# A frequency-domain mixing stage spread beside a feed-forward pipeline: two helper stages run further ahead, in finer steps, with two sums on another engine

## The chip, the cores and the metric

The kernel runs on one core of one Trainium2 chip. The core has a matrix engine (PE, TensorE), a vector engine (DVE, VectorE), an activation engine (ACT, ScalarE), a second elementwise engine (POOL, GpSimd) and a queue engine (SP, SyncE) that here only issues DMAs. Each engine works through its own instructions in the order in which the program gives them, and waits for the others through semaphores. The metric is the time on the device in microseconds, the median over several executions.

## The reference

The input x has 8 batches of 3008 rows and 256 columns. Each column is transformed along the rows, multiplied by a filter and transformed back; the result goes through two matrix products with x - tanh(x) between them.

```python
def _attn_ref(x, filt_r, filt_i):            # x (8, 3008, 256)
    X = np.fft.rfft(x, axis=1)
    F = (filt_r + 1j * filt_i)[None, :, :]   # (1505, 256)
    y = np.fft.irfft(X * F, n=x.shape[1], axis=1)
    return y.astype(np.float32)

def _moe_ref(x, w_in, w_out):                # x (24064, 256), w_in (256, 2048), w_out (2048, 256)
    h = x @ w_in
    g = h - np.tanh(h)
    return (g @ w_out).astype(np.float32)
```

## The kernel before

The transform of length 3008 = 64 x 47 is done in factors, as matrix products with constant matrices, and a batch goes through four stages:

- **first**, function `first`: 12 steps. A step loads two residues of x and the matrix f (SP queue), does 2 products on PE (line 296), copies the result out of PSUM on ACT (line 297) and stores it to the DRAM tensor ct1 (ACT queue). The loads of a step are asked for two steps ahead.
- **middle**, function `middle`: 7 slots. For a slot, `forth` does the 47-point transform (line 328, two pairs of products; the first pair is copied by ACT, the second is added to and subtracted from it on DVE, lines 333 and 334); `filtered` multiplies by the filter, with two products on POOL (lines 343 and 346), a difference and a sum into nn (lines 348 and 349), and a last sum and difference into xy (lines 351 and 352); `back` does the inverse 47-point transform (line 362, two pairs), copies each pair out on ACT (line 365) and stores it to the DRAM tensor ct2 (ACT queue). The slot's rows of ct1 (a2) and of the filter (ft) are loaded one slot ahead on SP. `back` of slot g is run within slot g+1.
- **last**, function `last`: per group of residues the final transform on PE (line 449, into pu), two copies by ACT, and four differences by `combine` (lines 463 to 466).
- **the feed-forward part**: 192 units U = 0 to 191; four units u = 0 to 3 make a group c = 0 to 5, six groups a batch p. Units are named c.u below. The two matrix products are done with seven products in place of eight. `up(U)` makes h in three PSUM banks x, y, z (line 483), from which DVE and ACT form the four blocks of h (lines 489, 506, 523, 531, 539); `shrink(U-1)` applies the approximated x - tanh(x) (ACT lines 554, 557, 565; DVE lines 561, 568) and the four differences t, on POOL, called t-combines (lines 463 to 466); `down(U-2)` does the second product (line 615) and, in each fourth unit, sums up the outputs, which are transposed on DVE (line 668) and stored by SP (line 695).

The order is written by hand: within a unit `up` calls back into `shrink`, `down` and, at five points, into t(k), k = 0 to 4. The point t(k) of unit c.u has the position 20c + 5u + k, so a batch has 120 positions. There one step of a helper stage is emitted on all engines at once: in units u = 3, at k = 0 and 2, a step of `last` for the next group; otherwise the next step of `first` or `middle` whose planned position has been reached. The t-combines of a unit are emitted between t(3) and t(4), just behind DVE's second line 568; DVE's line 539 stands behind t(4), line 506 behind the next unit's t(0), and the unit's first line 561 ahead of t(1).

While batch p runs, the plan puts first(p+1) at positions 0.24 to 32 and middle(p+1), in 51 steps, at 38 to 103. Batch 0's own first and middle stages run in a prologue that also converts weights; there the products of `filtered` are on DVE, its sums on POOL. The start of the next batch's loads and the two PSUM banks of the helper stages ("t", and "y" at k = 1, 2, 3) are set in the same loop.

Of the kernel before, what the change touches and what calls it, by code (L numbers as in the profile page):

```python
# [17 lines left out]
BATCH, SEQ, DM = 8, 3008, 256  # L18
# [8 lines left out]
NC = NH // CH  # L27
NX = NH // XH
SLOTS = [(a, min(SG, NA - a)) for a in range(0, NA, SG)]
KM = SG * NH  # L30
KL = SLOTS[-1][1] * NH
EARLY = 0

SMALL = 0.36
FACTORS = [(0.28138768672943115, 0.18210311233997345, 0.5012423992156982),
           (0.28138768672943115, -0.6558710336685181, 0.19358105957508087)]

FIRST, MID = (0.24, 32), (38, 103)

S, K = 0.6389930153911744, 0.3476472316053873  # L40
A, B = 0.18659689165196622, -0.6846325776203513
# [51 lines left out]
def kernel(  # L93
# [10 lines left out]
    V, G, ACT = nc.vector, nc.gpsimd, nc.scalar  # L104
# [232 lines left out]
    def filtered(g, xy, ft, by, by2):  # L337

        n = SLOTS[g][1] * NH
        ab = xy.rearrange("p (x v) c -> p x v c", v=2)  # L340
        fv = ft[0:n].rearrange("p (x v) c -> p x v c", v=2)
        nn = tr.tile([KM, 4, DM], F32, tag="nn", bufs=1, name="nn")[0:n]
        by.tensor_mul(nn.rearrange("p (x v) c -> p x v c", v=2), ab,  # L343
                      fv[:, :, 0:1].to_broadcast([n, 2, 2, DM]))
        yield
        by.tensor_mul(ab, ab, fv[:, :, 1:2].to_broadcast([n, 2, 2, DM]))  # L346
        yield
        by2.tensor_sub(nn[:, 0:4:3], nn[:, 0:4:3], xy[:, 1:3])  # L348
        by2.tensor_add(nn[:, 1:3], nn[:, 1:3], xy[:, 0:4:3])
        yield  # L350
        by2.tensor_add(xy[:, 0:2], nn[:, 0:2], nn[:, 2:4])  # L351
        by2.tensor_sub(xy[:, 2:4], nn[:, 0:2], nn[:, 2:4])  # L352
        yield

    def back(b, g, xy, z):
# [13 lines left out]
    def middle(b, z):  # L369

        a2, ft = {0: load_a2(b, 0)}, {0: load_ft(0)}
        waiting = iter(())
        yield
        for g in range(len(SLOTS)):
            if g + 1 < len(SLOTS):
                a2[g + 1], ft[g + 1] = load_a2(b, g + 1), load_ft(g + 1)
            there = forth(g, a2.pop(g), z)
            xy = next(there)
            yield
            next(there)  # L380
            done = filtered(g, xy, ft.pop(g), G, G)
            next(done)
            yield
            next(done)
            yield
            for _ in waiting:
                yield
            for _ in done:
                yield
            waiting = back(b, g, xy, z)  # L390
        yield
        yield
        for _ in waiting:
            yield
# [392 lines left out]
    with tc.tile_pool(name="tr", bufs=2) as tr, tc.manual_schedule():  # L787
        with tc.tile_pool(name="pro", bufs=1) as pro, \
# [81 lines left out]
            for g in range(last_g + 1):  # L870
# [3 lines left out]
                xy = next(there)  # L874
# [3 lines left out]
                done = filtered(g, xy, fts.pop(g), V, G)  # L878
# [6 lines left out]
                if g == last_g - 1:  # L885
                    fs = first(1, z1)
# [3 lines left out]
            for _ in waiting:  # L890
                pass
            e2s[0] = load_e2(*groups[0])
            for _ in range(EARLY):
                next(fs)
            for w in (ws, ws_gap):
                for _ in w:
                    pass
# [5 lines left out]
        with tc.tile_pool(name="dn", bufs=2) as dn, \  # L903
                tc.tile_pool(name="ps", bufs=1, space=bass.MemoryType.PSUM) as ps:

            quarter, latest = [1], ["t"]

            def zd(name, shape):
                latest[0] = "y" if quarter[0] in (1, 2, 3) and latest[0] == "t" else "t"
                return ps.tile(shape, F32, tag=latest[0], bufs=1, name=name)  # L910

            psums.append(zd)

            y_sums = dn.tile([128, 2 * 4 * len(groups)], F32, bufs=1, name="y_sums")

            def psl(shape, tag):
                return ps.tile(shape, F32, tag=tag, bufs=1, name="pt")

            def tiles1(k, dtype, n):

                tag, bufs = {"raw": ("ft", 2), "it": ("xy", 2), "pt": ("nn", 1), "st": ("e1", 2),
                             "ft": ("a2", 2)}[k]
                return tr.tile([128, n], dtype, tag=tag, bufs=bufs, name=k)

            def filters_d():
                zero = tr.tile([128, 2 * DM], F32, tag="a2", bufs=2, name="zero")
                G.memset(zero, 0.0)
                n = len(SLOTS) - 1
                nc.sync.dma_start(dram(filt_d, 2 * DM, [[KM * 4 * DM, n], [4 * DM, SG],
                                                        [1, 2 * DM]]), zero[0:n * SG])  # L930
                nc.sync.dma_start(dram(filt_d, (n * KM * 4 + 2) * DM, [[4 * DM, 1], [1, 2 * DM]]),
                                  zero[0:1])
                yield
                for g in range(len(SLOTS)):
                    for v, row, n, src in filter_rows(g):
                        G.dma_start(dram(filt_d, ((g * KM + row) * 4 + v) * DM,
                                         [[4 * DM, n], [1, DM]]), src)
                        yield

            bound = bounded()  # L940
            late, copies = weights_slow(tiles1, range(6, 8)), filters_d()
            total = 4 * len(groups)
            for _ in last(0, z1):
                pass
            next(late)
            for U in range(total + 2):
                i, u = divmod(U, 4)
                if U < total:
                    p, c = groups[i]
                    if c == 0 and u == 0:  # L950
                        steps, done = [], 0 if p else EARLY
                        if p + 1 < BATCH:
                            steps = [FIRST[0] + (FIRST[1] - FIRST[0]) * (k - done) / (NX - done)
                                     for k in range(NX)]
                            n_m = 7 * len(SLOTS) + 2
                            steps += [MID[0] + (MID[1] - MID[0]) * k / n_m for k in range(n_m)]
                            ms = None
                    if u == 0 and i + 1 < len(groups) and c + 1 < NC:
                        e2s[i + 1] = load_e2(*groups[i + 1])
                    if u == 2 and i + 1 < len(groups) and c + 1 == NC:  # L960
                        assert done == len(steps)
                        e2s[i + 1] = load_e2(*groups[i + 1])
                    if u == 0 and c + 1 == NC and p + 2 < BATCH:
                        fs = first(p + 2, z1)
                        next(fs)
                    if u == 2 and i + 1 < len(groups):
                        lasts = last(i + 1, z1)
                sh = shrink(U - 1) if 0 <= U - 1 < total else iter(())
                dw = down(U - 2) if 0 <= U - 2 < total else iter(())

                def d():

                    next(dw, None)

                def e():

                    next(dw, None)

                def s():

                    next(sh, None)

                def t(k):

                    nonlocal ms, done
                    quarter[0] = k
                    if k == 2 and stores:
                        store(*stores.pop())
                    store_some(4)
                    if U >= total:  # L990
                        return
                    pos = 20 * c + 5 * u + k
                    if u == 3 and k in (0, 2) and i + 1 < len(groups):
                        next(lasts)
                    elif done < len(steps) and steps[done] <= pos:
                        next(fs if done < NX else ms)
                        done += 1
                        if done == NX and ms is None:
                            ms = middle(p + 1, z1)
                            next(ms)  # L1000
                    next(late, None)
                    if k:
                        next(copies, None)

                if U < total:
                    if U == total - 1:
                        one = tr.tile([128, 128], F32, tag="x", bufs=3, name="one_sb")
                        nc.sync.dma_start(one, one_d)
                        ones = cst.tile([128, 1], F32, name="ones")
                        G.memset(ones, 1.0)  # L1010
                    up(U, d, e, s, t)
                else:
                    for k in range(5):
                        s()
                        s()
                        d()
                        if U == total + 1 and k in (0, 2):
                            next(bound)
                        e()
                        t(k)  # L1020
            for w in stores:
                store(*w)
            store_some(len(outs))
# [36 lines left out]
```

## Time and profile before

| | |
|---|---|
| median of 3 runs | 2919.11 us (2917.21 to 2925.43) |
| profiled execution, own time | 2923.08 us |
| its span | 2921.2 us |
| mean granted PE clock | 0.974 |
| instructions | 37028 |
| DMA moved | 215.48 MB, mean 74 GB/s |

The page gives the busy time of each engine and its share of the span, then the span in 40 equal slices with the busy share of each in tenths, and the chain of work that ended last. Views by line, by wait and by stretch of time come from the same trace. Line numbers are those of the kernel before; in the changed kernel the same lines stand a little lower or higher.

### The profile page before, as it was taken

What the parts mean: (1) busy time and instruction counts of PE and PEld (TensorE: products, weight loads), DVE (VectorE), ACT (ScalarE), POOL (GpSimd) and SP (SyncE); (2) the same over time, 40 slices, a digit from 0 to 9 for tenths busy, and PEclk for the clock granted to TensorE, in tenths of its full rate; (3) what the DMA queues carried; (4) which work ended last, traced back from release to release, by engine and by line L of the source; (5) the groups of instructions that cost most, each with busy time, mean ns of one, the idle gap of its engine ahead of it and who ended that gap; (6) DMA issues with size and microseconds to landing.
All of it is one profiled execution on the core that took longest, in us unless ns stands there. A gap on an engine that the chain in (4) does not pass through costs nothing.

```text
span 2921.2 us, 37028 instructions
## 1 busy us (share of the span) xinstructions
PE 2739.2 (94%) x12830; PEld 2373.4 (81%) x12830; DVE 2010.2 (69%) x2171; ACT 1764.4 (60%) x2583; POOL 2124.7 (73%) x1503
## 2 busy tenths in 40 slices
PE   4599999999999999999999999999999999999998
PEld 3388788988789887988779887898878988799886
DVE  5877766577665676657766677657776677677776
ACT  1156566666566665666656665666666666566665
POOL 5858995489944997559965699647995489855553
PEclk7699999999999999999999999999999999999999
DMA  9443322333123321233213322233322333111010
GB/s 249 117 151 89 76 54 53 101 81 81 42 63 98 91 63 42 76 103 73 58 40 100 91 66 58 52 107 73 80 58 52 103 73 84 26 28 35 19 26 17
DMA packets 341639, 215.48 MB, mean 74 GB/s; under 512 B 227736, under 2 KB 300988, under 8 KB 341251
## 3 DMA queue, kind: packets, MB, share of 16 engines
q1 hardware_dynamic: 296851, 154.15, 22.5%
q10 hardware_dynamic: 39504, 50.61, 5.5%
q0 software_dynamic: 5088, 8.28, 1.1%
q8 instruction: 103, 1.69, 0.3%
q14 instruction: 93, 0.76, 0.1%
HBM read 137.83 MB, written 78.12 MB: 74 GB/s over the span
## 4 chain that ended last, share of the span: by engine, by line
PE 50%; POOL 28%; DVE 10%; issue 5%; ACT 4%; DMA 2%; SPq 0%; ACTq 0%; POOLq 0%; DVEq 0%
PE o L615 21%; PE x L483 13%; PE z L483 6%; PE y L483 4%; POOL t L466 4%; DVE h L561 4%; POOL t L464 3%; POOL t L465 3%; POOL t L463 3%; POOL xy L346 2%; PE pf L296 2%; PE pu L449 2%; POOL nn L343 2%; POOL xy L352 2%; POOL nn L348 2%
## 5 line engine op out<-in xcount | busy, mean ns | idle before, releaser
L561 DVE TENSOR_TENSOR h<-h,y 128x1024 f32<-128x1024 f32 (+1 forms) x384 | 617.8, 1609 | 295.2 <-ACT y L557 295.2
L615 PE MATMUL o<-t,wd 128*128 128x256 f32 (+1 forms) x3072 | 790.4, 380 | 14.0 <-POOL t L465 7.1
L615 PEld LDWEIGHTS o<-t,wd 128*128 128x128 f32 x3072 | 586.8, 192 | 97.1 <-POOL t L465 13.7
L568 DVE SCALAR_TENSOR_TENSOR h<-sq,h 128x1024 f32<-128x1024 f32 (+1 forms) x384 | 595.7, 1551 | 99.2 <-ACT sq L565 93.2
L483 PE MATMUL x<-tu,wu 128*128 128x256 f32 (+1 forms) x2304 | 591.2, 379 | 3.1 <-ACT u L489 3.1
L615 PE MATMUL o<-h,wd 128*128 128x256 f32 (+1 forms) x2304 | 584.8, 376 | 4.6 <-DVE h L568 4.6
L463 POOL TENSOR_TENSOR t<-h 128x512 f32<-128x512 f32 (+1 forms) x190 | 245.3, 1291 | 444.4 <-DVE h L568 349.2
L483 PEld LDWEIGHTS x<-tu,wu 128*128 128x128 f32 x2304 | 435.9, 192 | 62.7 <-issue 7.9
L615 PEld LDWEIGHTS o<-h,wd 128*128 128x128 f32 x2304 | 433.7, 190 | 57.2 <-DVE h L568 8.3
L565 ACT ACTIVATE sq<-y,near_b 128x1024 f32<-128x1024 f32 (+1 forms) x384 | 435.1, 1133 | 9.2 <-DVE h L568 2.9
L554 ACT ACTIVATE y<-h 128x1024 f32<-128x1024 f32 (+1 forms) x384 | 397.5, 1035 | 13.3 <-ACT a L297 5.7
L557 ACT ACTIVATE y<-y 128x1024 f32<-128x1024 f32 (+1 forms) x384 | 399.7, 1041 | 6.3
L489 ACT COPY s<-x 128x512 f32<-128x512 f32 (+1 forms) x192 | 110.8, 577 | 424.8 <-PE x L483 424.4
L466 POOL TENSOR_TENSOR t<-t,h 128x512 f32<-128x512 f32 (+1 forms) x190 | 341.3, 1796 | 0.0
L489 ACT COPY u<-x 128x512 f32<-128x512 f32 (+1 forms) x384 | 220.7, 575 | 196.5 <-PE x L483 191.1
L465 POOL TENSOR_TENSOR t<-h 128x512 f32<-128x512 f32 (+1 forms) x190 | 277.6, 1461 | 0.0
L464 POOL TENSOR_TENSOR t<-h,t 128x512 f32<-128x512 f32 (+1 forms) x190 | 262.6, 1382 | 14.9
L523 DVE TENSOR_TENSOR h<-z,u 128x512 f32<-128x512 f32 (+1 forms) x192 | 128.5, 669 | 166.4 <-ACT u L489 165.8
L483 PE MATMUL x<-ut,wu 128*128 128x256 f32 (+1 forms) x768 | 202.2, 386 | 36.2 <-DVE h L531 35.0
L362 PE MATMUL pe<-xy,mats_sb 120*120 120x256 f32 (+1 forms) x448 | 132.6, 426 | 78.4 <-POOL xy L351 78.4
L483 PEld LDWEIGHTS x<-ut,wu 128*128 128x128 f32 x768 | 139.7, 191 | 76.2 <-DVE h L531 61.2
L506 DVE TENSOR_TENSOR h<-y,s 128x512 f32<-128x512 f32 (+1 forms) x192 | 130.1, 677 | 99.0 <-PE y L483 93.8
(116 smaller groups left out, 3688.7 us busy)
## 6 DMA issues: line engine op xcount, KB each, us to landing
e<-ct SPq DMA_DIRECT2D x48, 512.0 KB, 4.8
a<-ct SPq DMA_DIRECT2D x48, 480.0 KB, 4.9
ct<-e ACTq DMA_DIRECT2D x96, 240.0 KB, 2.5
ct<-a ACTq DMA_DIRECT2D x84, 256.0 KB, 3.1
x_sb<-in_x_dram SPq DMA_DIRECT2D x161, 128.0 KB, 3.3
ft<-filt SPq DMA_DIRECT2D x42, 480.0 KB, 6.3
out_dram<-ot SPq DMA_DIRECT2D x1248, 16.0 KB, 1.5
gt<-g SPq DMA_DIRECT2D x48, 256.0 KB, 3.2
```

Source lines behind the costliest of these rows:

```text
L463: by.tensor_sub(t[0], b[0][1], b[0][0])
L464: by.tensor_sub(t[1], b[1][1], t[0])
L465: by.tensor_sub(t[2], b[1][1], b[0][1])
L466: by.tensor_sub(t[3], t[1], b[1][0])
L483: nc.tensor.matmul(bank[:, k], wu[:, q - 1, (2 * u + k) * 128:(2 * u + k + 1) * 128], rhs[q - 1], start=(first and k == 0), stop=True, ski ...
L489: ACT.copy(t, X)
L554: ACT.activation(y[k], ht[k], AF.Arctan, scale=S)
L557: ACT.activation(y[k], y[k], AF.Square, accum_out=y_sums[:, 2 * U + k // 2:2 * U + k // 2 + 1])
L561: V.tensor_mul(ht[k], ht[k], y[k])
L565: ACT.activation(sq[k], y[k], AF.Square, bias=near_b, scale=A)
L568: V.scalar_tensor_tensor(out=ht[k], in0=sq[k], scalar=K, in1=ht[k], op0=ALU.add, op1=ALU.mult)
L615: nc.tensor.matmul(product(q), wd[:, q - 1, (2 * u + k) * 128: (2 * u + k + 1) * 128], rhs[q - 1][:, k], start=(u == 0 and k == 0 and q == ...
```

## The change

Both helper stages run one batch further ahead in part. While batch p runs, first(p+2) and middle(p+1) are both spread evenly over positions 0.2 to 102; while batch 0 runs, first(1) takes positions 0.2 to 15, first(2) 15 to 30, and middle(1) 30 to 102. The steps of both are merged in order of position, and one is emitted at a point. `middle` gets a further pause in each slot, between the sum and difference of `forth` and the first product of `filtered`, and one more in the last slot; one pause behind the last slot goes: 58 steps in place of 51. The last sum and difference of `filtered` are done on DVE, in the stages and in the prologue. The generators of the stages to come are made, and their first loads asked for, at position 105 of batch p, for middle(p+2) and first(p+3).

```diff
@@ filtered
         by2.tensor_sub(nn[:, 0:4:3], nn[:, 0:4:3], xy[:, 1:3])
         by2.tensor_add(nn[:, 1:3], nn[:, 1:3], xy[:, 0:4:3])
         yield
-        by2.tensor_add(xy[:, 0:2], nn[:, 0:2], nn[:, 2:4])
-        by2.tensor_sub(xy[:, 2:4], nn[:, 0:2], nn[:, 2:4])
+        V.tensor_add(xy[:, 0:2], nn[:, 0:2], nn[:, 2:4])
+        V.tensor_sub(xy[:, 2:4], nn[:, 0:2], nn[:, 2:4])
         yield
@@ middle
             next(there)
+            yield
             done = filtered(g, xy, ft.pop(g), G, G)
             next(done)
             yield
             next(done)
             yield
             for _ in waiting:
+                yield
+            next(done)
+            yield
+            if g + 1 == len(SLOTS):
                 yield
             for _ in done:
                 yield
             waiting = back(b, g, xy, z)
-        yield
         yield
         for _ in waiting:
             yield
@@ the plan
-FIRST, MID = (0.24, 32), (38, 103)
+LEAD, LAG = 30, 102
...
-                        steps, done = [], 0 if p else EARLY
-                        if p + 1 < BATCH:
-                            steps = [FIRST[0] + (FIRST[1] - FIRST[0]) * (k - done) / (NX - done)
-                                     for k in range(NX)]
-                            n_m = 7 * len(SLOTS) + 2
-                            steps += [MID[0] + (MID[1] - MID[0]) * k / n_m for k in range(n_m)]
-                            ms = None
+                        steps = planned(p)
...
+            def planned(p):
+                def spread(n, lo, hi, *what):
+                    return [(lo + (hi - lo) * k / n, *what, k) for k in range(n)]
+                n_m = 8 * len(SLOTS) + 2
+                f = [spread(NX, *((0.2, LEAD / 2) if b == 1 else (LEAD / 2, LEAD) if b == 2
+                                  else (0.2, LAG)), firsts, b, first)
+                     for b in ([1, 2] if p == 0 else [p + 2]) if b < BATCH]
+                m = [spread(n_m, LEAD if p == 0 else 0.2, LAG, mids, b, middle)
+                     for b in [p + 1] if b < BATCH]
+                return sorted(sum(f + m, []), key=lambda s: s[0])
...
-                    if u == 0 and c + 1 == NC and p + 2 < BATCH:
-                        fs = first(p + 2, z1)
-                        next(fs)
+                    if u == 1 and c + 1 == NC:
+                        for gens, ahead, what in ((mids, 2, middle), (firsts, 3, first)):
+                            if p + ahead < BATCH:
+                                gens[p + ahead] = what(p + ahead, z1)
+                                next(gens[p + ahead])
...
-                    elif done < len(steps) and steps[done] <= pos:
-                        next(fs if done < NX else ms)
-                        done += 1
-                        if done == NX and ms is None:
-                            ms = middle(p + 1, z1)
-                            next(ms)
+                    elif steps and steps[0][0] <= pos:
+                        _, gens, b, what, n = steps.pop(0)
+                        if b not in gens:
+                            gens[b] = what(b, z1)
+                            next(gens[b])
+                        next(gens[b])
```

More of the change, by code (lines that the diff above doesn't have):

```diff
@@ L31 @@
 KL = SLOTS[-1][1] * NH
-EARLY = 0
 SMALL = 0.36
@@ L892 @@
             e2s[0] = load_e2(*groups[0])
-            for _ in range(EARLY):
-                next(fs)
             for w in (ws, ws_gap):
@@ L945 @@
             next(late)
+            def planned(p):
[8 more added lines that the diff above has]
+                return sorted(sum(f + m, []), key=lambda s: s[0])
+            firsts, mids = {1: fs}, {}
             for U in range(total + 2):
@@ L960 @@
                     if u == 2 and i + 1 < len(groups) and c + 1 == NC:
-                        assert done == len(steps)
+                        assert not steps
                         e2s[i + 1] = load_e2(*groups[i + 1])
-                    if u == 0 and c + 1 == NC and p + 2 < BATCH:
-                        fs = first(p + 2, z1)
-                        next(fs)
+                    if u == 1 and c + 1 == NC:
[3 more added lines that the diff above has]
+                                next(gens[p + ahead])
                     if u == 2 and i + 1 < len(groups):
@@ L983, in t @@
                 def t(k):
-                    nonlocal ms, done
                     quarter[0] = k
```

## The prediction

> **What bounds the kernel now.** I read the page first: busy shares, slices, chain.
>
> ```profile
> span 2921.2 us, 37028 instructions
> ...
> PE 2739.2 (94%) x12830; PEld 2373.4 (81%) x12830; DVE 2010.2 (69%) x2171; ACT 1764.4 (60%) x2583; POOL 2124.7 (73%) x1503
> ...
> POOL 5858995489944997559965699647995489855553
> ...
> PE 50%; POOL 28%; DVE 10%; issue 5%; ACT 4%; DMA 2%; SPq 0%; ACTq 0%; POOLq 0%; DVEq 0%
> ```
>
> PE is busy almost throughout, yet the chain that ended last runs on POOL for 28% of the span. POOL's digits go up to 9 once per batch. So I cut the span at the copy of line 531, which DVE makes once in each of the 192 units: batch 0, batch 1, batch 6, batch 7 (to its last copy).
>
> ```profile
> 156.20:511.20 355.00, 333.78 (x1563) 287.52 (x1564) 255.63 (x274) 217.14 (x318) 285.88 (x215) 0.99 0.31 79
> 511.20:860.10 348.90, 337.62 (x1602) 293.78 (x1601) 237.35 (x250) 219.51 (x322) 262.76 (x174) 0.99 0.29 73
> ...
> 2258.50:2606.70 348.20, 336.92 (x1598) 293.16 (x1597) 238.21 (x250) 218.97 (x321) 262.80 (x174) 0.99 0.28 68
> 2606.70:2890.80 284.10, 283.56 (x1370) 252.60 (x1369) 211.37 (x228) 191.33 (x275) 162.71 (x125) 1.00 0.11 23
> ```
>
> The columns after the length are PE, PEld, DVE, ACT and POOL busy, granted clock, DMA share, GB/s. Batches 1 to 6 take (2606.70 - 511.20) / 6 = 349.3 each. Batch 7 has no first or middle stage beside it and shows what a batch costs without them. The same view by groups of four units: five groups of batch 2, its group 4, five groups of batch 7, its group 4.
>
> ```profile
> 860.10:1155.90 295.80, 284.54 (x1352) 247.71 (x1351) 201.58 (x211) 184.61 (x271) 234.93 (x152) 0.99 0.31 76
> 1089.60:1155.90 66.30, 59.31 (x265) 48.44 (x266) 43.89 (x43) 37.45 (x54) 59.08 (x36) 0.97 0.18 41
> 2606.70:2854.05 247.35, 246.87 (x1201) 220.69 (x1200) 181.97 (x196) 166.50 (x240) 142.19 (x110) 1.00 0.12 24
> 2803.60:2854.05 50.45, 50.40 (x241) 44.19 (x240) 37.03 (x40) 33.93 (x49) 29.25 (x22) 1.00 0.08 11
> ```
>
> A bare batch is 247.35 + 50.45 = 297.8, with PE never idle. In group 4 of batch 2 PE idles 7 of 66.30 us and POOL works 59.08. Its late middle stage waits for POOL:
>
> ```profile
> 1494.45 0.59 PE L615 MATMUL o<-t,wd 128*128 128x256 f32 x2
> 1498.52 1.58 PE L362 MATMUL pe<-xy,mats_sb 48*48 48x256 f32 x4 [3.48 <-POOL xy L351]
> ...
> 1508.44 0.81 PE L483 MATMUL z<-ut,wu 128*128 128x256 f32 x3
> ```
>
> PE stood still 3.48 us until POOL's sum of line 351, and was then slow. Undisturbed, four matmuls follow the next four after 0.86 us (z at 2804.05, x at 2804.91, rows further down), 0.216 each.
>
> ```profile
> L296 PE MATMUL pf<-x_sb,f 128*128 128x256 f32 x336 | 87.9, 384 | 1.0 <-DVE h L506 0.7 <-ACT a L297 0.2
> ...
> L362 PE MATMUL pe<-xy,mats_sb 120*120 120x256 f32 (+1 forms) x448 | 132.6, 426 | 78.4 <-POOL xy L351 78.4
> ```
>
> A first stage is 336 / 7 = 48 matmuls, a middle stage 448 / 8 = 56 in line 362 and by the code as many in line 328. At 0.216 that is 10.4 and 24.2, so PE needs 297.8 + 34.6 = 332.4 for a full batch and 349.3 - 332.4 = 17 are lost. Between 1498.52 and 1508.44 PE ran 28 matmuls, worth 6.0 us, in 9.9: this one event costs 3.48 + 3.9 = 7.4. It is in every batch, since it is in the order of the code.
>
> **The change part by part.** Middle work on POOL and DVE:
>
> ```profile
> L343 POOL TENSOR_TENSOR nn<-xy,ft 120x1024 f32<-120x1024 f32 x42 | 122.7, 2922 | 7.6 <-DVE xy L334 6.0
> L346 POOL TENSOR_TENSOR xy<-xy,ft 120x1024 f32<-120x1024 f32 x42 | 117.8, 2805 | 2.1
> ...
> L352 POOL TENSOR_TENSOR xy<-nn 120x512 f32<-120x512 f32 x48 | 82.5, 1719 | 0.0
> L348 POOL TENSOR_TENSOR nn<-nn,xy 120x512 f32<-120x512 f32 x48 | 82.2, 1711 | 12.5 <-DVE xy L346 12.0
> L351 POOL TENSOR_TENSOR xy<-nn 120x512 f32<-120x512 f32 x48 | 81.7, 1701 | 2.6
> L349 POOL TENSOR_TENSOR nn<-nn,xy 120x512 f32<-120x512 f32 x48 | 75.7, 1577 | 0.0
> ...
> L333 DVE TENSOR_TENSOR xy<-pa,xy 120x512 f32<-120x512 f32 x48 | 32.8, 682 | 25.6 <-PE pa L328 24.4
> ```
>
> A slot (seven per batch) costs POOL 12.4 now; the two last sums, 1.70 + 1.72 = 3.4, go to DVE. POOL falls from 262.8 to 239 of some 341 us. The steps go from 65 of a batch's 120 positions to 102, so POOL's load is level: about 40 of each 57 us group, nearer to batch 7's 29 of 50 than to 59 of 66. No form like the new DVE sums is in the stages of the trace; line 333 (0.68, one operand from PSUM) is nearest, the POOL row is the far end. I take 0.69: 7 x 1.4 = 9.7 us of DVE per batch, which is 68% busy, so beside PE's work unless DVE has to wait.
>
> Line 362 needs the sums of a slot five steps later, at 1.76 positions each about 25 us. So the 7.4 go, and with them a good part of the other 9.6 lost beside POOL at its limit; I keep 4 (ends 1 and 8). What is late next is DVE: its sums now wait for line 349, and DVE runs in order. From the plan's numbers I placed the seven pairs. In five slots POOL reaches lines 348 and 349 well before DVE reaches the sums. In slot 5 of batches 1 to 5 POOL's pair falls at the last position of a unit, behind the four t-combines, and DVE's at the first position of the next, ahead of line 506. A bare unit, to lay this on:
>
> ```profile
> 2793.63 1.28 POOL L463 TENSOR_TENSOR t<-h 128x512 f32<-128x512 f32 x1 [2.96 <-DVE h L568]
> ...
> 2797.45 2.25 POOL L466 TENSOR_TENSOR t<-t,h 128x512 f32<-128x512 f32 x1
> ...
> 2792.28 1.21 DVE L568 SCALAR_TENSOR_TENSOR h<-sq,h 128x1024 f32<-128x1024 f32 x1
> 2793.41 0.68 DVE L539 TENSOR_TENSOR h<-z,u 128x512 f32<-128x512 f32 x1
> 2794.85 0.69 DVE L506 TENSOR_TENSOR h<-y,s 128x512 f32<-128x512 f32 x1 [0.77 <-PE y L483]
> 2796.64 1.93 DVE L561 TENSOR_TENSOR h<-h,y 128x1024 f32<-128x1024 f32 x1 [1.10 <-ACT y L557]
> ...
> 2801.41 0.69 DVE L523 TENSOR_TENSOR h<-z,u 128x512 f32<-128x512 f32 x1 [0.63 <-ACT u L489]
> 2802.46 1.23 DVE L561 TENSOR_TENSOR h<-h,y 128x1024 f32<-128x1024 f32 x1 [0.36 <-ACT y L557]
> 2803.60 0.68 DVE L531 COPY h<-x 128x512 f32<-128x512 f32 x1
> ...
> 2804.05 1.03 PE L483 MATMUL z<-ut,wu 128*128 128x256 f32 x4
> 2804.91 1.03 PE L483 MATMUL x<-ut,wu 128*128 128x256 f32 x4
> ```
>
> POOL's combines end at 2799.70; 1.71 + 1.58 more is 2803.0, and DVE, there since 2794.1, adds until 2804.4. Then lines 506, 561, 568, 523, 561, 531 at 0.69, 1.23, 1.21, 0.69, 1.23, 0.68 end line 523 at 2808.2 and line 531 at 2810.1. PE's z wants the first at 2804.05 and x the second at 2804.91: 5.2 late, less the two extra PE steps of that unit (1.7), 3.5; with DVE silent POOL can run at 1.28 an operation, so I take 3 (ends 1.5 and 5.2). Slot 4 of batches 1 to 6 has POOL's pair in the same place and DVE's behind the first line 561 (ends 2798.57): line 523 then ends near 2806.3 and line 531 at 2808.2, against z at 2805.8 and x at 2806.6 with the extra steps: 2 (ends 0.6 and 3). ACT, queued for DVE's h, shares these stalls and adds none.
>
> A rule speaks against sums on DVE. The quoted line 561 took 1.93 us beside POOL's work and 1.23 without. The Trainium skill (SBUF — State Buffer, "SBUF: two separate sides") says that a DVE operation with two SBUF inputs and a GpSimd one lock each other out of a shared port pair for the whole instruction, which those two rows fit. By it each new sum could wait out one POOL operation, 1.7 us, twice in slots 4 and 5: 11 x 3.4 = 37 us more.
>
> The moved loads and stores:
>
> ```profile
> SPq L695 <- DVE ot L668: 1122.5, 47, 42.7
> ...
> PE pe L362 <- POOL xy L351: 44.7, 7, 9.1
> ```
>
> The first row is SP's queue: it waits 1122.5 us in all for output transposes, up to 42.7 at once, and now more x, f, a and ft loads stand behind those waits. They are asked for two first-steps (17 positions, 48 us) or one slot (14 positions, 40 us) ahead, so I cost this nothing; without that cover a load costs up to its wait. In batch 0 the prefetch is only 2.5 positions, but the first output store comes after those loads in the queue. The second row is PE's wait before 145 us, the prologue, where the sums move too: DVE halves their time but idles during lines 348 and 349. I take -3 (ends -6 and +4).
>
> The sum. Batches 1 to 5: 332.4 + 4 + 3 + 2 = 341.4 each, 1707. Batch 6 has no first stage left: 297.8 + 24.2 + 6 = 328. Batch 0 gets both: 297.8 + 20.8 + 24.2 = 342.8, and it lost 355.0 - 332.4 = 22.6, of which I take off 7.4 and 3 that dense first steps fill: 355. Together 2390 against 2606.70 - 156.20 = 2450.5: -60.5, with the prologue -63.5. The profiled execution took 2923.08 us (2921.2 span), 4 above the median 2919.11; taken from the median: **2855**.
>
> **The rivals.** *PE drops to the slow rate again.* After 3.48 us of idling PE lost 3.9; slot 5's first gap is 2.5 to 4.2, so it may do so there. With that and both stalls at their upper ends: 5 x (3.9 + 2.2 + 1) + 1 = 36.5 more, 2892. For it: the size of the gap; against: extra PE steps shorten it. Chance 0.20. The Trainium skill (TensorE: Matmul & The Clock Gate, "What's actually happening") puts the fall to half clock after an idle window of about 3.4 us, free-running; the 3.48 row agrees.
>
> *Slower: DVE queues behind POOL in every slot.* If each pair of sums costs the 3 us of slot 5: 42 x 3 in batches 1 to 6 less the 5 x 3 + 6 x 2 counted, and 21 in batch 0, is 120 more, 2975. It decides from (63.5 + 27) / 49 = 1.85 us a slot. For it: steps are now only one or two positions from pair to sums; against: a unit gives POOL some 4 us of rest. Chance 0.13.
>
> *It doesn't do what it says.* If the 17 us belong to the units' own ACT and DVE chain, spreading only spreads them: batches 1 to 5 stay 349.4, batch 6 falls by 10.4 and batch 0 rises by as much: 2919. For it: line 531 delays PE without POOL too; against: group 4's POOL row. Chance 0.07.
>
> **How the numbers follow.** Forecast 0.60, own range 2825 to 2885. All low ends together (losses 3.1 in batches 1 to 5) give about 2812, all high ends (16) about 2913. The range 2815 to 2918 holds the forecast and the first rival. A measurement of this kernel tells 0.3%, 9 us, from no change: faster 0.60 + 0.20 = 0.80; the third rival is the same, 0.07; slower 0.13.
>
> **What would show it.** Right: batches 1 to 5 near 341, batch 6 near 328, no wait of line 362's matmuls for sums in these batches, POOL without slices of 9 and near 239 per batch, DVE waits of some 4 to 9 us for POOL's second difference in slots 4 and 5 only. Wrong: batches 1 to 5 at 347 or more; DVE waiting on POOL in most slots; slow matmuls after a PE gap each batch; PE waiting for loads in batch 0.

## The result, and the profile after

The changed kernel takes 2908.74 us (median of 5 runs, 2903.64 to 2909.29) against 2922.98 us of the kernel before (median of 5): the ratio is 0.995, with a 95% interval of 0.9934 to 0.9965. It is faster by 14 us, where 64 were forecast: less than a quarter of the expected gain. The profiled execution took 2905.42 us.

From the page of the changed kernel: span, busy times, POOL's slices and the engines of the chain that ended last.

```profile
span 2903.6 us, 36938 instructions
...
PE 2730.1 (94%) x12830; PEld 2376.1 (82%) x12830; DVE 2067.3 (71%) x2283; ACT 1762.8 (61%) x2583; POOL 1897.8 (65%) x1391
...
POOL 4557886767657776666666766576675777655553
...
PE 65%; DVE 13%; POOL 11%; issue 4%; ACT 3%; DMA 2%; SPq 0%; ACTq 0%; DVEq 0%; POOLq 0%
```

POOL is level now, without a 9, and its share of the chain fell from 28% to 11%. PE's share of the span has stayed at 94%. The view by stretches of time, cut at the same copies (line 534 now), shows batch 0, batch 1, batch 6 and batch 7:

```profile
154.00:509.50 355.50, 340.54 (x1615) 295.92 (x1616) 264.50 (x289) 223.29 (x330) 260.03 (x201) 1.00 0.41 107
509.50:858.10 348.60, 337.43 (x1602) 295.07 (x1601) 246.64 (x264) 219.28 (x321) 231.97 (x160) 0.99 0.29 73
2251.00:2590.40 339.40, 327.03 (x1546) 285.17 (x1545) 253.22 (x261) 211.87 (x309) 241.04 (x160) 0.98 0.19 44
2590.40:2874.70 284.30, 283.68 (x1369) 252.49 (x1368) 209.25 (x227) 191.31 (x276) 162.65 (x125) 1.00 0.11 23
```

The prologue is 2.2 us shorter (first copy at 154.0, before at 156.2), batch 0 is 355.5. Batches 1 to 5 take (2251.0 - 509.5) / 5 = 348.3 each, only 1 less than before, though POOL works 30 us less in each; batch 6 takes 339.4. So the wait of PE for POOL's sums went, and something else came in its place. The list of waits of batch 2 (858 to 1206) names it: waited for, us in total, times, longest.

```profile
DVE xy L350 <- POOL nn L348: 13.6, 4, 6.6
...
PE pa L327 <- DVE h L509: 7.5, 2, 5.0
```

The longer of PE's two waits, in order of time on POOL, DVE and PE (line 509 is the former 506, 542 the former 539, 327 the former 328, 350 and 351 the two sums that moved):

```profile
873.58 1.59 POOL L645 TENSOR_TENSOR o<-pu,x 128x256 f32<-128x256 f32 x1
874.63 1.78 PE L618 MATMUL o<-h,wd 128*128 128x224 f32 x8
874.84 0.61 DVE L542 TENSOR_TENSOR h<-z,u 128x448 f32<-128x448 f32 x1
875.13 1.28 POOL L347 TENSOR_TENSOR nn<-nn,xy 120x512 f32<-120x512 f32 x1
876.36 1.26 POOL L348 TENSOR_TENSOR nn<-nn,xy 120x512 f32<-120x512 f32 x1
877.65 1.60 DVE L350 TENSOR_TENSOR xy<-nn 120x512 f32<-120x512 f32 x1 [2.21 <-POOL nn L348]
879.18 1.61 DVE L351 TENSOR_TENSOR xy<-nn 120x512 f32<-120x512 f32 x1
880.71 0.61 DVE L509 TENSOR_TENSOR h<-y,s 128x448 f32<-128x448 f32 x1
881.38 2.06 PE L327 MATMUL pa<-a,mats_sb 120*120 120x256 f32 x4 [4.96 <-DVE h L509]
883.23 1.61 PE L486 MATMUL x<-tu,wu 128*128 128x224 f32 x4
884.68 0.92 PE L486 MATMUL z<-tu,wu 128*128 128x224 f32 x4
```

This is slot 0's pair of sums, at t(0) of unit 0.2. DVE waits only 2.21 us for POOL, adds for 3.2 us, and only then reads PSUM bank y in line 509. At the next point, t(1), slot 1's first transform (line 327) has been given that same bank y, so PE, which runs in order, stands for 4.96 us; then its first four matmuls take 1.85 us in place of 0.86, the next four 1.45 in place of 0.76. Together 4.96 + 0.99 + 0.69 = 6.6 us. The second stall follows slot 2's sums (t(4) of unit 1.3, helper at t(1) of unit 2.0).

```profile
964.90 1.75 DVE L350 TENSOR_TENSOR xy<-nn 120x512 f32<-120x512 f32 x1 [1.16 <-POOL nn L348]
...
968.85 0.68 DVE L509 TENSOR_TENSOR h<-y,s 128x512 f32<-128x512 f32 x1
...
969.58 1.72 PE L327 MATMUL pa<-a,mats_sb 120*120 120x256 f32 x4 [2.49 <-DVE h L509]
971.09 1.91 PE L486 MATMUL x<-tu,wu 128*128 128x256 f32 x4
972.80 1.31 PE L486 MATMUL z<-tu,wu 128*128 128x256 f32 x4
```

DVE waits 1.16 us there and adds for 3.4. The stall costs 2.49 and, from 969.58 to 973.95 for 12 matmuls worth 2.6, some 1.8 more. The trace holds its own counterexample: DVE's longest wait for POOL in that batch, 6.61 us for slot 5, stops PE hardly at all: no idle time of PE over 0.2 us follows it.

```profile
1087.17 1.06 PE L327 MATMUL pa<-a,mats_sb 48*48 48x256 f32 x4
...
1091.13 0.69 DVE L350 TENSOR_TENSOR xy<-nn 120x512 f32<-120x512 f32 x1 [6.61 <-POOL nn L348]
...
1092.34 0.69 DVE L509 TENSOR_TENSOR h<-y,s 128x512 f32<-128x512 f32 x1
```

There the helper's matmul at t(1) ran at 1087.17, five microseconds before line 509: it had the other bank, t. So it is not the length of DVE's wait that decides, but what PE wants from DVE behind it.

### The profile page after: what moved, and what is told of

Its sections match the earlier page's. It is cut to its first block, busy times and chain, and to the rows that moved or that the text cites. A ratio compares the mean times of both kernels' runs of the same rounds, so it can differ in the third digit from the quotient of the medians.

```text
span 2903.6 us, 36938 instructions
## 1 busy us (share of the span) xinstructions
PE 2730.1 (94%) x12830; PEld 2376.1 (82%) x12830; DVE 2067.3 (71%) x2283; ACT 1762.8 (61%) x2583; POOL 1897.8 (65%) x1391
## 3 DMA queue, kind: packets, MB, share of 16 engines
q8 instruction: 103, 1.69, 0.3%
## 4 chain that ended last, share of the span: by engine, by line
PE 65%; DVE 13%; POOL 11%; issue 4%; ACT 3%; DMA 2%; SPq 0%; ACTq 0%; DVEq 0%; POOLq 0%
PE o L618 26%; PE x L486 17%; PE z L486 8%; PE y L486 4%; DVE h L564 4%; PE pu L452 3%; PE pe L361 3%; DVE h L571 2%; PE pa L327 2%; PE pf L295 2%; POOL nn L347 2%; POOL nn L348 2%; ACT y L560 2%; POOL t L469 2%; DVE xy L351 1%
## 5 line engine op out<-in xcount | busy, mean ns | idle before, releaser
L564 DVE TENSOR_TENSOR h<-h,y 128x1024 f32<-128x1024 f32 (+1 forms) x384 | 598.1, 1558 | 288.0 <-ACT y L560 287.4
L618 PE MATMUL o<-t,wd 128*128 128x256 f32 (+1 forms) x3072 | 776.0, 375 | 0.0
L466 POOL TENSOR_TENSOR t<-h 128x512 f32<-128x512 f32 (+1 forms) x190 | 240.7, 1267 | 604.1 <-DVE h L571 371.2
L469 POOL TENSOR_TENSOR t<-t,h 128x512 f32<-128x512 f32 (+1 forms) x190 | 351.9, 1852 | 0.0
L467 POOL TENSOR_TENSOR t<-h,t 128x512 f32<-128x512 f32 (+1 forms) x190 | 245.9, 1294 | 14.9
L468 POOL TENSOR_TENSOR t<-h 128x512 f32<-128x512 f32 (+1 forms) x190 | 244.8, 1288 | 0.0
L486 PE MATMUL z<-tu,wu 128*128 128x256 f32 (+1 forms) x768 | 196.7, 379 | 3.4 <-DVE h L542 3.4
L486 PE MATMUL z<-ut,wu 128*128 128x256 f32 (+1 forms) x768 | 194.4, 375 | 1.1 <-DVE h L526 1.0
```

Of the source, the lines that this page charges most:

```text
L466: by.tensor_sub(t[0], b[0][1], b[0][0])
L467: by.tensor_sub(t[1], b[1][1], t[0])
L468: by.tensor_sub(t[2], b[1][1], b[0][1])
L469: by.tensor_sub(t[3], t[1], b[1][0])
L486: nc.tensor.matmul(bank[:, k], wu[:, q - 1, (2 * u + k) * 128:(2 * u + k + 1) * 128], rhs[q - 1], start=(first and k == 0), stop=True, ski ...
L564: V.tensor_mul(ht[k], ht[k], y[k])
```

## The experiments

The theory (A): PE stops because a helper's matmul at t(1) needs bank y, which line 509 empties only behind the new sums. The rivals: POOL's relief brought the gain and the order costs little (B); the loss is the units' own (C); DVE's added work is what costs, wherever it stands in the order (the DVE-load rival).

**e1: the sums back on POOL**, all else as changed.

```diff
-        V.tensor_add(xy[:, 0:2], nn[:, 0:2], nn[:, 2:4])
-        V.tensor_sub(xy[:, 2:4], nn[:, 0:2], nn[:, 2:4])
+        by2.tensor_add(xy[:, 0:2], nn[:, 0:2], nn[:, 2:4])
+        by2.tensor_sub(xy[:, 2:4], nn[:, 0:2], nn[:, 2:4])
```

> The changed kernel with one part undone: the last sum and difference of the filter go back to POOL; both stages stay spread, with the finer steps. Theory A (the two long PE stalls of each batch, after 5.24 and 2.65 us gaps, come from DVE's line 509 standing behind the new DVE sums while PE wants the helper bank y): without sums on DVE both stalls go, some 11 us in each of batches 1 to 6, so about 2908.7 - 66 = 2843, unless PE then waits for POOL's sums again. Rival B (POOL's relief of 24 us a batch is what brought the gain, and DVE's order costs little): POOL is back at 262 us a batch, the 7.4 us event of the kernel before returns in each, about 2908.7 + 40 = 2950. Rival C (the loss of some 16 us a batch belongs to the units, however the helpers are placed): no change, 2900 to 2915.

2862.39 us, ratio to the kernel before 0.9799 (0.9778 to 0.9819). The new plan alone (the even spread, the finer steps and the first stage run further ahead, which this run does not tell apart) is worth 2%, and the sums on DVE took three quarters of that away again. The gaps that the expectation gives as 5.24 and 2.65 us are the 4.96 and 2.49 of the rows above. Batch 0, batch 2 and batch 6 of e1, by stretches:

```profile
155.00:518.90 363.90, 342.01 (x1614) 296.04 (x1613) 260.54 (x275) 224.24 (x330) 284.25 (x215) 0.99 0.40 104
857.80:1195.10 337.30, 333.41 (x1602) 292.80 (x1601) 246.45 (x250) 219.40 (x322) 264.17 (x174) 1.00 0.30 75
2211.90:2541.90 330.00, 322.99 (x1546) 281.77 (x1545) 246.85 (x248) 212.00 (x309) 269.42 (x174) 1.00 0.20 46
```

POOL works 264 us in batch 2, as much as in the kernel before, and the batch takes 337.3 in place of 348 (batches 1 to 5: 338.6 on average): B falls, and so does C. POOL's work did not have to become less; placed by the new plan, it no longer holds PE up in these batches. Only batch 0, where the steps are still dense, pays for the sums on POOL: 363.9 against 355.5, with one event like the one of the kernel before.

```profile
455.21 1.94 PE L361 MATMUL pe<-xy,mats_sb 48*48 48x256 f32 x4 [5.60 <-POOL xy L350]
```

**e2: the DVE sums never at t(4) or t(0).** `SUMS` holds the numbers of those steps in the middle stage.

```diff
-                    elif steps and steps[0][0] <= pos:
+                    elif steps and steps[0][0] <= pos and not (
+                            k in (0, 4) and steps[0][3] is middle and steps[0][4] in SUMS):
```

> The changed kernel, but the DVE sums are not emitted at the points t(4) and t(0) of a unit: a step of sums that falls there waits for t(1), behind line 509 and the first line 564. Everything else keeps its plan, later steps move by a point or two. Theory A: the two stalls of PE on bank y go, 2908.7 - 60 = about 2849, the waits of DVE for line 348 get shorter. Rival B (DVE has simply more to do, 2067 us busy in place of 2010, and its sums take 1.6 us beside POOL): no change, 2903 to 2913. Rival C: no change.

2861.67 us, ratio 0.9792 (0.977 to 0.9813): as theory A said, within 13 us of its number. Batch 2 takes 340.7, and the waits of DVE for POOL fall from 13.6 to 7.2 us. DVE does as much as in the changed kernel, so its load alone does not explain the loss.

**e3: no helper tile in bank y at t(1).** The sums stay where they were.

```diff
-                latest[0] = "y" if quarter[0] in (1, 2, 3) and latest[0] == "t" else "t"
+                latest[0] = "y" if quarter[0] in (2, 3) and latest[0] == "t" else "t"
```

> The changed kernel, but a helper stage may take PSUM bank y only at t(2) and t(3), at t(1) always bank t. Theory A in its narrow form (what stops PE is the bank alone: line 509 must have read y before the helper's matmul at t(1)): PE's waits for line 509 go and with them most of 11 us a batch, about 2855, though DVE still waits as long for line 348. Theory A in its wide form (DVE's whole chain is late, so PE stops a little later for x or z): a third of that or less, 2890 to 2905. Rival C: no change or slower, since bank t is then reused sooner.

2862.95 us, ratio 0.9803 (0.9783 to 0.9823). From e3, batch 2: the waits, the stretch, and the timeline of the place where the changed kernel has its long stall.

```profile
DVE xy L350 <- POOL nn L348: 13.6, 4, 6.6
```

```profile
847.80:1188.60 340.80, 334.63 (x1602) 292.43 (x1601) 250.23 (x264) 219.41 (x321) 234.64 (x160) 1.00 0.30 75
```

```profile
865.94 1.03 PE L327 MATMUL pa<-a,mats_sb 120*120 120x256 f32 x4
...
866.81 0.92 PE L486 MATMUL x<-tu,wu 128*128 128x224 f32 x4
...
867.35 1.61 DVE L350 TENSOR_TENSOR xy<-nn 120x512 f32<-120x512 f32 x1 [2.21 <-POOL nn L348]
...
870.43 0.61 DVE L509 TENSOR_TENSOR h<-y,s 128x448 f32<-128x448 f32 x1
```

DVE waits for POOL to the tenth of a microsecond as in the changed kernel (13.6 in all, 6.6 at most) and line 509 is as late, but PE goes through at 865.94, ahead of it. The batch takes 340.8. This run and its control, e8 below, settle the cause for batches 1 to 5: the waits of DVE for POOL cost PE little here, the bank behind them cost the rest. Beside e8, which has the same bank rule and the sums on POOL, the sums on DVE still cost 2.4 us a batch (340.8 against 338.4). The wide form of theory A, which expected 2890 or more, falls for these batches; in batch 6 it holds once, since a PE wait of 3.35 us for DVE's line 542 (bank z), behind a pair of sums, stays in e3.

**e6: both cures together.** The edits of e2 and e3.

> The changed kernel with both cures, sums not at t(4) and t(0), and no bank y at t(1). Theory A: both take away the same stall, so the second adds little: 2855 to 2864, batches 1 to 5 near 340. If they were two losses, they would add up: 2908.7 - 47 - 46 = 2816.

2860.29 us, ratio 0.9796 (0.9779 to 0.9813): no more than either alone. They take away the same stall.

**e4: the sums on DVE in the old plan.** The kernel before, with only this part of the change.

```diff
-        by2.tensor_add(xy[:, 0:2], nn[:, 0:2], nn[:, 2:4])
-        by2.tensor_sub(xy[:, 2:4], nn[:, 0:2], nn[:, 2:4])
+        V.tensor_add(xy[:, 0:2], nn[:, 0:2], nn[:, 2:4])
+        V.tensor_sub(xy[:, 2:4], nn[:, 0:2], nn[:, 2:4])
```

> The kernel before with one part of the change alone: the last sum and difference on DVE, in the stages and in the prologue, the old plan (middle stage at positions 38 to 103). Theory A: the 3.48 us wait of PE for POOL's sum and the slow matmuls behind it go (7.4 us a batch), but some of the seven pairs bring DVE stalls like those of the changed kernel: 2919 - 52 + 0 to 60, so 2870 to 2930. Rival B: POOL's 24 us a batch are worth all, 2919 - 52 - 7 x 5 = about 2832. Rival C: 2915 to 2925.

2977.04 us, ratio 1.0185 (1.0167 to 1.0204): slower by 53 us than the kernel before beside it (2924.47), beyond every number expected, although POOL is relieved by 32 us a batch. Its waits in batch 2, and the worst of the three PE waits:

```profile
DVE xy L351 <- POOL nn L349: 20.6, 5, 8.4
...
PE pa L328 <- DVE h L506: 10.3, 3, 4.2
```

```profile
1072.70 2.06 PE L328 MATMUL pa<-a,mats_sb 120*120 120x256 f32 x4 [4.23 <-DVE h L506]
1074.55 1.91 PE L483 MATMUL x<-tu,wu 128*128 128x256 f32 x4
1076.26 2.43 PE L615 MATMUL o<-t,wd 128*128 128x256 f32 x8
```

The same link, three times a batch.

**e5, e9, e10: how far the bank is the link in the old plan.** All three are e4 with one more edit: e5 the bank rule of e3; e9 helper tiles only in bank t; e10 the sums not at t(4) and t(0).

> The kernel before with the sums on DVE (as in e4, old plan) and the rule of e3 (no helper tile in bank y at t(1)). Theory A, narrow: in e4 PE waits three times a batch for line 506, 2.79 to 4.23 us, each with slow matmuls behind it, some 18 us a batch; without the bank these go although DVE waits for POOL as long: 2977 - 7 x 15 = about 2870. Theory A, wide (DVE's lateness reaches PE over x and z anyway): a third, 2940. Rival B' (DVE sums are harmful by DVE's load): no change, 2965 to 2980.

2959.43 us, ratio 1.0131 (1.0114 to 1.0148), 18 us less than e4 (14, if each is taken against the kernel before beside it); 2870 was a miss, and the time lies nearest to rival B'. Of the three waits for line 506 two stayed (7.5 us in batch 2): with DVE held up for 7.5 and 8.4 us, line 506 is late even for a helper that takes bank y at t(2).

> The kernel before with the sums on DVE (e4, old plan), and helper tiles never in bank y, only in bank t. In e5 two of e4's three PE waits for line 506 stayed: there the helper's matmul in bank y stood at t(2). Theory A, narrow: with no helper in bank y there is no PE wait for line 506 at all, about 14 us a batch less than e5 if the freed PE doesn't stop elsewhere: 2860 to 2900, at the price of bank t being reused sooner. Theory A, wide (a DVE wait of 7 to 8 us reaches PE over x or z anyhow): 2930 to 2960. Rival (DVE's load): 2950 to 2975.

2949.73 us, ratio 1.0096 (1.0079 to 1.0113). No wait for line 506 is left, but others of PE take its place; from e9's waits of batch 2:

```profile
DVE xy L351 <- POOL nn L349: 20.5, 5, 8.3
PE x L483 <- DVE h L531: 7.0, 8, 1.8
PE z L483 <- DVE h L523: 3.1, 2, 2.5
PE z L483 <- DVE h L539: 2.4, 2, 1.9
```

So in the dense plan the wide form holds by the waits: with DVE held up for 7 to 8 us in a unit, PE stops for x and z as well. The time alone would not tell, since it lies at the edge of the rival's range too.

> The kernel before with the sums on DVE, but not at t(4) and t(0), old plan, bank y as before. Theory A: with line 506 ahead of the sums PE's waits for it go; DVE's waits for POOL become shorter, since the later point gives POOL time: 2850 to 2890. Rival (DVE's load, or the sums' mere presence, in the dense part): 2940 or more.

2927.83 us, ratio 1.0026 (1.0015 to 1.0036), 49 us less than e4 (45, each against the kernel before beside it) and still a little slower than the kernel before. The place of the sums makes most of their price there too; but 2850 to 2890 was a miss. DVE still waits 15.6 us a batch for POOL, now ahead of lines 569 and 524 (the former 568 and 523), and batches 1 to 6 take 349 to 353 us again. For the old plan the sums on DVE are no gain in any of the four forms tried.

**e7 and e8: the parts that paid, together.** The sums go to DVE in the prologue and in batch 1's middle stage, which runs beside the dense batch 0, and stay on POOL for all later batches; e8 has the bank rule of e3 as well. The new last argument of `filtered` is the engine of the two sums.

```diff
-            done = filtered(g, xy, ft.pop(g), G, G)
+            done = filtered(g, xy, ft.pop(g), G, G, V if b == 1 else G)
```

> The changed kernel with the sums on DVE in the prologue and for batch 1's middle stage (run beside batch 0, where steps are dense), and on POOL for all later batches; bank y as in the changed kernel. From the pieces: start 152 to 154, batch 0 as in the changed kernel 355.5, batches 1 to 6 as in e1 338.8 and 330.0: 2908.7 - 5 x 9.5 - 9.4 = about 2852. Theory A expects this sum; if POOL's load matters in batches 1 to 6 (rival B), the gain is lost there.

> As e7 with the rule of e3. Where no sums stand on DVE there is nothing for line 509 to wait behind, so theory A expects the bank rule to add only what it does in batch 0: 2848 to 2854. If the rule helps by itself, whatever DVE does, it takes several us more off each batch: below 2835.

2847.67 us, ratio 0.9753 (0.9736 to 0.9771), and 2844.80 us, ratio 0.9743 (0.9725 to 0.976). The sum of the pieces, 2852, was right to 5 us, and the bank rule adds nothing that the intervals tell apart. That is the control for e3: where no sums stand ahead of line 509, taking bank y away at t(1) brings nothing, so its gain in e3 was the link and not the other banks that the helpers then get. Both beat the kernel before by 2.5% and the changed one by 2%. Batch 2 of e8, its stretch and the longest entry of PE's waits in it:

```profile
849.20:1188.00 338.80, 333.54 (x1601) 292.71 (x1600) 245.30 (x249) 219.36 (x322) 262.22 (x174) 1.00 0.31 75
```

```profile
PE x L486 <- DVE h L534: 3.8, 5, 1.2
```

Five short waits for the copy out of bank x are the most that is left.

**e11: e8 without the finer steps.**

```diff
             next(there)
-            yield
             done = filtered(g, xy, ft.pop(g), G, G, V if b == 1 else G)
...
-                n_m = 8 * len(SLOTS) + 2
+                n_m = 7 * len(SLOTS) + 2
```

> e8 without the finer steps: the pause between DVE's pair of line 332 and the first product is taken out, 51 steps for the middle stage. Theory A (only what stands behind what matters, not the step's size): within 8 us of e8, 2837 to 2853. If the pause is needed (POOL's first product waits for DVE and holds up the t-combines), 10 us or more slower: 2855 or more.

2864.63 us, ratio 0.9808 (0.9791 to 0.9824): 20 us slower than e8, so the finer step is worth something. Half of it is in batch 0 (365.0 against 355.5) and 6 in batch 6. The reason that the expectation named is not the one: POOL's wait for DVE's pair in batch 0 is 5.4 us against 5.1 in e8. Since all later steps change their points as well, whether it is the step's size or where the steps fell is left open.

## Why the prediction was wrong, point by point

- **What bounds the kernel, and the bare batch: right.** Batch 7 is unchanged (284.3 against 284.1 us), and the 332.4 us that PE needs for a full batch fit batches 1 to 5 of e1: 338.6 on average, with 6.2 lost, inside the ends 1 and 8 that the prediction gave to what it took as 4.
- **The event of 7.4 us a batch goes: right.** In the stages of the changed kernel PE waits for no sum in line 361. The price was read from the dearest of seven events: behind the same gap of 3.5 us the slow matmuls cost 2.2 to 3.9 us in the kernel before, 3.9 in the row that was priced. POOL's forecast of 239 us a batch came out at 232.
- **Batch 0 and the prologue: right in number**, 355.5 us against 355, and -2.2 against -3. But PE waited three times for loads of x in batch 0 (line 295), 3.8 us in all and up to 1.8, which the prediction had put at nothing; that the total fits all the same is in part luck. No PE wait of note for loads appeared in batches 1 to 6.
- **What is late next: the step that failed.** "In five slots POOL reaches lines 348 and 349 well before DVE reaches the sums" was read as harmless for all five. In slots 0 and 2 POOL was only 2.21 and 1.16 us behind, but DVE's own 3.2 to 3.4 us of adding came on top, and it stood ahead of line 506 while PE's next helper needed bank y. I looked at what PE wants from lines 523 and 531 and at nothing else that PE wants from DVE; the alternation of the helpers' banks stood in the code. Priced from the rows: 6.6 and 4.3 us, 10.9 in each of batches 1 to 5; taking the bank away (e3) gave back 348.3 - 340.8 = 7.5, taking the sums off DVE (e1) 348.3 - 338.6 = 9.7. With the link cut (e3) the batches take 340.8, against the forecast 341.4, and the whole kernel 2863 against 2855. That agreement is of the sum and not of its terms, so partly luck: of the forecast's 4 + 3 + 2 the 3 and the 2 stood for slots 4 and 5, which cost less.
- **Slots 4 and 5: priced too high.** DVE waited there for 3.6 and 6.6 us, as placed, but PE's longest idle time behind them was 1.3 to 1.4 us for slot 4 and 0.2 us for slot 5; I had priced 2 and 3. POOL ran at 1.27 us an operation there, as the prediction allowed for; that the slack of the extra PE steps was larger than counted is likely, but no run shows it.
- **The price of a sum on DVE: too low.** I took 0.69 us; in the changed kernel the two take 0.97 and 1.11 on average, 1.60 to 1.75 beside POOL's work and 0.69 without (the rows at 877.65 and 1091.13). The Trainium skill's lock on the shared port pair (SBUF — State Buffer, "SBUF: two separate sides"), which I cited and priced but left out of the sum, is what these two rows look like; in slots 0 and 2 the two sums took 3.2 and 3.4 us in place of 1.4, a third to a half of the time by which line 509 was late. The prediction had priced it for slots 4 and 5, where POOL was silent during the sums and they took 0.69 us.
- **Batch 6: 339.4 against 328.** Two such stalls again, one over bank y behind slot 5's sums and one over z behind slot 0's (2.8 and 3.4 us, each with slow matmuls behind it); e3 takes away the first (333.3), e1 both (330.0).
- **The rivals.** The slow rate after a PE gap did come back, at slots 0 and 2 instead of 5. The slower rival (DVE queues behind POOL in every slot) is what e4 comes nearest to, in the old plan: 53 us slower. In the new plan DVE waited for POOL in four slots of seven (2.2, 1.2, 3.6 and 6.6 us), and two of these stopped PE for long. The third (the 17 us belong to the units' own chain) falls with e1, where batches 1 to 5 take 338.6.
- **The range and the signs.** The time lies inside the stated range, but not by its reasons: 348.3 - 332.4 = 15.9 us a batch were lost, as with all high ends (16), yet half of that upper sum stood for slots 4 and 5, and the runs put most of the loss in slots 0 and 2. The ends given add up to about 2818 and 2903 rather than 2812 and 2913; the rest would have to be batch 0's, for which no ends are given. All four signs named for "wrong" came: 348.3 a batch, DVE waiting in four slots of seven, slow matmuls behind a PE gap in each batch, and PE waiting for loads in batch 0.

## What to carry to other kernels

A sum moved to an idler engine was paid for here not by that engine's load but by what stood behind it in its order: before moving it, list every buffer, the shared PSUM banks above all, that the engine empties next, and who on the bounding engine wants each of them. The new plan of the helpers' steps, spread evenly and finer, was worth 2% with no work taken off any engine; taking 30 us of work a batch off the loaded one was worth nothing more where the steps were even. When two parts of a change come together, measure them apart: here one gave 2% and the other took most of it.

## What the runs showed of the hardware

PE can fall to half rate after shorter gaps than the 3.48 us of the kernel before: 2.49 us at 969.58 was enough (four matmuls in 1.51 and 1.71 us in place of 0.86; the granted clock of the 4 us from there is 0.57). The Trainium skill (TensorE: Matmul & The Clock Gate, "What's actually happening") speaks of an idle window of about 3.4 us, free-running; in these runs the fall is seen behind shorter gaps too, and the length of the gap alone does not decide. In the kernel before, the same gap of 1.69 us stands in each of batches 1 to 6: twice the clock fell behind it (0.54 from 1348.55 to 1350.80), four times it did not (1.00 from 1000.59 to 1002.80). In e5 a gap of 3.29 us at 1104.87 was followed by the full clock, 1.00 for the next 2.9 us. Where the clock fell behind the gap of 2.49 us, that cost 1.8 us each time, so such a gap is priced at 2.49 to 4.3 us; behind the 3.5 us of the kernel before it cost 2.2 to 3.9 us.
